# Engine streams written straight into the program, without a block, and the last store waited for last

## The chip, the cores and the metric

The kernel runs on one core of a Trainium2 chip. The metric is the device time of one execution in microseconds. It covers more than the kernel's own instructions: the profiled execution of the kernel before has a span of 169.3 us from its first to its last instruction and a time of 171.16 us.

Three words are used throughout. The *last landing* is the last increment of the semaphore that the last store raises. The *tail* is the time from the last landing to the last record of semaphore 2. No line of the kernel touches semaphore 2; the trace shows its changes before the first and after the last instruction of the program. The *body* is everything up to the last landing.

## The reference

```python
B, H, S, D = 1, 32, 2048, 128            # q, k, v in bfloat16

def reference(q, k, v):
    phi_q = jnp.where(q > 0, q + 1, jnp.exp(q)) + 1e-6
    phi_k = jnp.where(k > 0, k + 1, jnp.exp(k)) + 1e-6
    kv = jnp.einsum("bhsd,bhse->bhde", phi_k, v)
    z = jnp.einsum("bhsd->bhd", phi_k)
    num = jnp.einsum("bhqd,bhde->bhqe", phi_q, kv)
    den = jnp.einsum("bhqd,bhd->bhq", phi_q, z)[..., None] + 1e-6
    return num / den
```

## The kernel before

It works head by head, 32 heads. SyncE issues every load and store. TensorE transposes q, multiplies; ScalarE takes exponentials; VectorE clips, divides and scales; GpSimd does a share of the clipping and copies v. Each operation carries a list of operations that it needs, and a small scheduler turns these into waits on semaphores. For the change only the end matters: how the five lists of instructions get into the program, and what SyncE waits for at last.

```python
NO = 12                                   # output buffers, one semaphore each

def emit(self, eng, engine):
    for fn, waits, name, by in self.plan[eng]:
        for s, v in waits:
            engine.wait_ge(self.get(s), v)
        ins = fn(engine)
        if by:
            ins.then_inc(self.get(name), by)

# ... (head h stores from buffer h % NO and raises semaphore o{h % NO})
        block = es.enter_context(nc.Block())

        @block.gpsimd
        def _(e):
            pr.emit("POOL", e)

        @block.sync
        def _(e):
            pr.emit("SP", e)
            for s in range(NO):
                if f"o{s}" in pr.count:
                    e.wait_ge(pr.get(f"o{s}"), pr.count[f"o{s}"])

        @block.scalar
        # ... and so for TensorE and VectorE
```

## Time and profile before

| | before |
|---|---|
| time, median of the first 3 runs | 171.89 us (171.8 to 172.0) |
| span of the profiled execution | 169.3 us |
| TensorE matmul, VectorE, ScalarE busy | 94%, 91%, 91% of the span |
| DMA: share of the stores' and loads' queue | 98.5% of 16 engines |
| last landing | 168.53 us |
| end of the last instruction | 169.26 us |
| last record of semaphore 2 | 171.17 us |
| tail | 2.64 us |

The first rows say that the body is full and that nothing in it is changed. The last four are read from single records of the trace, since the page rounds to 0.1 us. The lines of the profile are shown with the prediction. In them SP is SyncE, PE TensorE (PEld its weight loads), DVE VectorE, ACT ScalarE and POOL GpSimd; a q behind the name is the engine's sequencer. An EVENT_SEMAPHORE is an instruction that only waits for semaphores or changes them.

### The profile page before, as it was taken

Reading aid. Unit: us, or ns where it says so; the run is one execution under the profiler, and the core shown is the slowest. Engines: PE = TensorE matmul, PEld = TensorE weight load, DVE = VectorE, ACT = ScalarE, POOL = GpSimd, SP = SyncE. Lnnn points to the kernel's source line nnn. Section 1 sums busy time; section 2 is a strip of 40 time slices with the busy share of each in tenths; the row PEclk is TensorE's granted clock in tenths of the full one; section 3 lists DMA queues with packets and bytes.
Section 4 is the critical chain, followed back from the end, with each engine's and each line's share of the span. In section 5 each row is a group of like instructions: output and inputs, shape, how many; then the busy total and the mean of one; then the engine's idle time right before and its main releaser. Section 6 shows DMA issues by size and latency. Waiting matters only on the chain.

```text
span 169.3 us, 6317 instructions
## 1 busy us (share of the span) xinstructions
PE 158.8 (94%) x2775; PEld 153.5 (91%) x2775; DVE 153.5 (91%) x267; ACT 153.7 (91%) x133; POOL 85.8 (51%) x71
## 2 busy tenths in 40 slices
PE   6997999999999999999999999999999999999850
PEld 2576989999999999999999999999999999999740
DVE  0178989999999999999999999999999999999891
ACT  3799989999999999999999999999999999995800
POOL 1446546655665456545566555554565555635000
PEclk9999999999999999999999999999999999999999
DMA  5999999999999999999999999999999999999984
GB/s 204 394 420 415 403 407 410 406 410 410 413 410 410 410 411 407 410 408 419 411 415 417 413 423 411 411 419 408 415 417 414 417 413 419 415 412 420 391 342 175
DMA packets 18748, 67.53 MB, mean 399 GB/s; under 512 B 2080, under 2 KB 2464, under 8 KB 18720
## 3 DMA queue, kind: packets, MB, share of 16 engines
q1 hardware_dynamic: 18720, 67.12, 98.5%
q8 instruction: 22, 0.36, 0.8%
q14 instruction: 6, 0.05, 0.1%
HBM read 50.33 MB, written 16.78 MB: 396 GB/s over the span
## 4 chain that ended last, share of the span: by engine, by line
PE 86%; DVE 6%; ACT 4%; issue 1%; DVEq 0%; POOL 0%; POOLq 0%
PE la L357 33%; PE la L394 19%; PE la L396 17%; PE la L368 15%; DVE la L410 4%; ACT la L336 2%; PE la L315 2%; ACT la L372 1%; PE la L389 1%; DVE la L374 1%; DVE la L403 1%; ACT la L378 1%; DVE la L342 0%; DVEq L253 0%; ACT la L362 0%
## 5 line engine op out<-in xcount | busy, mean ns | idle before, releaser
L410 DVE TENSOR_TENSOR la<-la 128x1536 bf16<-128x1536 f32 (+2 forms) x65 | 77.6, 1195 | 0.3
L396 PE MATMUL la<-la 128*128 128x129 bf16 x512 | 68.1, 220 | 0.0
L394 PE MATMUL la<-la 128*128 128x129 bf16 x512 | 68.1, 219 | 0.0
L372 ACT ACTIVATE la<-la 128x2048 bf16<-128x2048 bf16 (+2 forms) x35 | 60.4, 1731 | 5.0 <-PE la L368 3.3
L357 PE MATMUL la<-la 128*128 128x129 bf16 x1024 | 64.0, 219 | 0.0
L336 ACT ACTIVATE la<-la 128x2048 bf16<-128x2048 bf16 (+1 forms) x33 | 61.3, 1861 | 0.0
L350 POOL COPY la<-la 128x1024 int32<-128x1024 int32 (+1 forms) x33 | 40.3, 1223 | 40.1 <-DVE la L403 30.5
L357 PEld LDWEIGHTS la<-la 128*128 128x128 bf16 x1024 | 60.0, 97 | 0.5 <-POOL la L350 0.5
L346 POOL TENSOR_SCALAR la<-la 128x1024 bf16<-128x1024 bf16 x32 | 44.9, 1403 | 28.2 <-DVE la L410 24.2
L396 PEld LDWEIGHTS la<-la 128*128 128x128 bf16 x512 | 49.5, 97 | 0.0
L394 PEld LDWEIGHTS la<-la 128*128 128x128 bf16 x512 | 47.1, 97 | 0.0
L389 PE MATMUL la<-la 128*128 128x3 bf16 (+1 forms) x192 | 32.3, 168 | 3.4 <-DVE la L410 1.9
L368 PE MATMUL la<-la 128*128 128x128 bf16 x512 | 33.7, 219 | 0.0
L378 ACT ACTIVATE la<-la 128x1024 bf16<-128x1024 bf16 (+1 forms) x32 | 33.5, 1046 | 0.0
L368 PEld LDWEIGHTS la<-la 128*128 128x128 bf16 x512 | 29.2, 97 | 0.9 <-DMA la<-in_q_dram 0.2
L339 DVE TENSOR_SCALAR la<-la 128x2048 bf16<-128x2048 bf16 (+1 forms) x33 | 23.5, 716 | 3.1 <-ACT la L336 3.0
L389 PEld LDWEIGHTS la<-la 128*128 128x128 bf16 x192 | 18.7, 97 | 4.4 <-DVE la L410 2.3
L374 DVE TENSOR_SCALAR la<-la 128x2048 bf16<-128x2048 bf16 (+2 forms) x35 | 21.9, 625 | 0.1
L381 DVE TENSOR_SCALAR la<-la 128x1024 bf16<-128x1024 bf16 x31 | 20.8, 672 | 0.2 <-ACT la L372 0.2
L342 DVE TENSOR_SCALAR la<-la 128x1024 bf16<-128x1024 bf16 x32 | 14.2, 447 | 5.3 <-DMA la<-in_k_dram 5.3
L403 DVE RECIPROCAL la<-la 128x12 f32<-128x12 f32 (+2 forms) x65 | 12.8, 198 | 2.9 <-ACT la L362 1.0
L362 ACT ACTIVATE la<-la 128x129 bf16<-128x129 f32 x32 | 9.0, 282 | 0.8 <-PE la L357 0.8
(14 smaller groups left out, 11.7 us busy)
## 6 DMA issues: line engine op xcount, KB each, us to landing
la<-in_q_dram SPq DMA_DIRECT2D x32, 512.0 KB, 15.4
la<-in_k_dram SPq DMA_DIRECT2D x32, 512.0 KB, 15.3
la<-in_v_dram SPq DMA_DIRECT2D x32, 512.0 KB, 15.4
out_dram<-la SPq DMA_DIRECT2D x31, 512.0 KB, 15.3
out_dram<-la SPq DMA_DIRECT2D x2, 192.0 KB, 2.8
out_dram<-la SPq DMA_DIRECT2D x1, 128.0 KB, 3.0
```

What stands on the lines that cost most here:

```text
L336: add("ACT", f"ek{h}.{i}", lambda e, a=a, b=b: e.activation(em_sb[:, h % NE, a:b], k_sb[:, h % NI, a:b], ACT.Exp), over("ldk", h, ld_parts ...
L346: add("POOL", f"rkp{h}.{i}", lambda e, a=a, b=b: e.tensor_scalar(rk_sb[:, h % NR, a:b], k_sb[:, h % NI, a:b], BIG, 0.0, op0=ALU.min, op1=A ...
L350: add("POOL", f"v1{h}.{i}", lambda e, a=a, b=b: e.tensor_copy(v1_sb[:, h % NV, a:b, 0:D].bitcast(i32), v_sb[:, h % NI, a:b].bitcast(i32)), ...
L357: ins = e.matmul(kv_ps, lhsT=src[:, j], rhs=v1_sb[:, h % NV, j, 0:NC], start=(j + part == 0), stop=(j == NT - 1 and part == 1))
L368: ins = e.transpose(xT[:, j], q_sb[:, h % NI, j], ident[:])
L372: add("ACT", f"eq{h}.{i}", lambda e, a=a, b=b: e.activation(emq_sb[:, h % NQ, a:b], xT[:, a:b], ACT.Exp), over("T", h, t_parts, a, b) + fr ...
L374: add("DVE", f"emq{h}.{i}", lambda e, a=a, b=b: e.tensor_scalar(emq_sb[:, h % NQ, a:b], emq_sb[:, h % NQ, a:b], 1.0, EPS, op0=ALU.min, op1 ...
L378: add("ACT", f"rqa{h}", lambda e: e.activation(rq_sb[:, h % NQ, 0:n], xT[:, 0:n], ACT.Relu), over("T", h, t_parts, 0, n) + freed(NQ, h, (" ...
L389: e.matmul(_ap(o_ps[:, :], o + D, [[NC, m]]), lhsT=ones[:], rhs=epsr[:, 0:m], start=True, stop=False, skip_group_check=True)
L394: e.matmul(to, lhsT=emq_sb[:, h % NQ, t], rhs=kvs_sb[:, h % NK], start=False, stop=False, skip_group_check=True)
L396: ins = e.matmul(to, lhsT=rq_sb[:, h % NQ, t], rhs=kvs_sb[:, h % NK], start=False, stop=True, skip_group_check=True)
L410: return e.tensor_tensor(out=_ap(o_sb[:, :, :, :], first(o_sb[:, h % NO, t0, 0:1]) - first(o_sb[:, :, :, :]), [[m * D, nb], [D, m], [1, D] ...
```

## The change

The intent: a block ends with a drain on each engine, a branch and a barrier of all five engines, and these stand behind the last store. Without a block there is none of it. And since SyncE has to see all twelve output semaphores anyway, the one that comes last is put last.

```diff
-        block = es.enter_context(nc.Block())
-
-        @block.gpsimd
-        def _(e):
-            pr.emit("POOL", e)
-
-        @block.sync
-        def _(e):
-            pr.emit("SP", e)
-            for s in range(NO):
-                if f"o{s}" in pr.count:
-                    e.wait_ge(pr.get(f"o{s}"), pr.count[f"o{s}"])
-        ... (ScalarE, TensorE and VectorE in the same way)
+        for e, engine in (("POOL", nc.gpsimd), ("SP", nc.sync), ("ACT", nc.scalar), ("PE", nc.tensor), ("DVE", nc.vector)):
+            pr.emit(e, engine)
+        last = f"o{(NH - 1) % NO}"
+        for name in [f"o{s}" for s in range(NO) if f"o{s}" in pr.count and f"o{s}" != last] + [last]:
+            nc.sync.wait_ge(pr.get(name), pr.count[name])
```

More of the change, by code (lines that the diff above doesn't have):

```diff
@@ L430, in bass_standalone__linear_attn_elu__prompt_kernel @@
             pr.get(name)
-        block = es.enter_context(nc.Block())
-        @block.gpsimd
-        def _(e):
-            pr.emit("POOL", e)
-        @block.sync
-        def _(e):
-            pr.emit("SP", e)
-            for s in range(NO):
-                if f"o{s}" in pr.count:
-                    e.wait_ge(pr.get(f"o{s}"), pr.count[f"o{s}"])
-        @block.scalar
-        def _(e):
-            pr.emit("ACT", e)
-        @block.tensor
-        def _(e):
-            pr.emit("PE", e)
-        @block.vector
-        def _(e):
-            pr.emit("DVE", e)
+        for e, engine in (("POOL", nc.gpsimd), ("SP", nc.sync), ("ACT", nc.scalar), ("PE", nc.tensor), ("DVE", nc.vector)):
[3 more added lines that the diff above has]
+            nc.sync.wait_ge(pr.get(name), pr.count[name])
 _INS = ['q', 'k', 'v']
```

## The prediction

> **What bounds the kernel now.** I read the page first for the body of the run, then the end of the chain of work, the source views of the two lines that the change deletes, and the run's last microseconds record by record.
>
> ```profile
> span 169.3 us, 6317 instructions
> ...
> PE   6997999999999999999999999999999999999850
> ...
> DVE  0178989999999999999999999999999999999891
> ...
> DMA  5999999999999999999999999999999999999984
> GB/s 204 394 420 415 403 407 410 406 410 410 413 410 410 410 411 407 410 408 419 411 415 417 413 423 411 411 419 408 415 417 414 417 413 419 415 412 420 391 342 175
> ```
>
> The slices of 4.23 us show matmul and the DMA engines at nine tenths from the second slice to about the 37th. Both are full, and the change touches neither. What it touches lies in the last slice, where only stores and waits are left. The chain of waits for the stretch from 162.5 us ends so:
>
> ```profile
> 162.84 0.96 DVE la L410
> 163.80 0.24 DVE la L403 x2
> 164.04 0.86 DVE la L410
> 164.89 0.59 DVEq L253
> ```
>
> The chain stops on VectorE's own drain (L253 is the line of the kernel under which everything at the block's exit is filed) at 165.5 us and does not reach 169.3. So this view does not explain the last 3.8 us: it follows compute, and these 3.8 us are a transfer and semaphore traffic. SyncE's waits and the source views of lines 442 (the wait for the stores) and 253 have them:
>
> ```profile
> SPq L442 <- DMA out_dram<-la: 2.6, 2, 1.3
> ```
> ```profile
> L442 SPq EVENT_SEMAPHORE  x6: 17/28/28, 167.2 to 168.8; - x6
> ```
> ```profile
> L253 POOLq EVENT_SEMAPHORE  x2: 17/17/17, 169.1 to 169.2; - x2
> L253 POOLq DRAIN  x1: 1744/1744/1744, 153.1 to 153.1; - x1
> L253 ACTq DRAIN  x1: 2134/2134/2134, 158.1 to 158.1; - x1
> L253 PEldq DRAIN  x1: 1123/1123/1123, 162.7 to 162.7; - x1
> L253 DVEq DRAIN  x1: 1455/1455/1455, 164.1 to 164.1; - x1
> L253 SPq COMPARE_BRANCH  x1: 38/38/38, 168.9 to 168.9; - x1
> L253 SPq DRAIN  x1: 7/7/7, 169.0 to 169.0; - x1
> L253 SPq EVENT_SEMAPHORE  x1: 17/17/17, 169.2 to 169.2; - x1
> ```
>
> SyncE sits in two waits of 1.3 us, one for head 30's store and one for head 31's. Then come more event semaphores, one branch, a short drain, and the barrier. The four other engines' drains start at 153.1 to 164.1 us and last 1.1 to 2.1 us: all are over by 165.5 us, three microseconds before the last store is in. They look large and cost nothing.
>
> The single records give the tail in ns. The last of the 48 increments of the last store's semaphore comes at 168.532. SyncE's wait that contains it runs 168.549 to 168.577. Four more event semaphores start at 168.622, 168.686, 168.747 and 168.807 (two semaphores each, all long satisfied), the branch, which carries the twelfth wait, at 168.874, the drain at 169.044. GpSimd collects at 169.077 and releases at 169.155; SyncE's last event is 169.197 to 169.214 and TensorE's ends last, at 169.260. The span ends there, but the time doesn't: the profiled run's time is 171.16, and semaphore 2, which no line of the kernel owns, goes on changing: nine records from 169.498 to 170.030 and nine from 170.817 to 171.174, with the clearing of semaphores one after the other between them. So a postamble of 171.174 - 169.260 = 1.91 us follows the kernel and belongs to the time.
>
> **What the Trainium skill says.** "Runtime: NRT & Kernel Launch", section "The ~15µs preamble/postamble breakdown", lists a sync_barrier after the kernel, a clearing of the semaphores and a second sync_barrier, and describes the barrier as a serpentine over five engines at about 44 ns a hop, 355 ns in all. The trace agrees: the nine records before the kernel's first instruction span 0.371 us, those of the second barrier after it 0.357. The first after it takes 0.532, because its second step is 0.212 where the same step elsewhere is 0.038: one engine came late by about 0.17 us. So the program's own barrier is doubled by one that the runtime adds.
> "DMA: Bandwidth & Descriptors", section "Anatomy of one DMA — SWDGE (gpsimd) path", puts most of a transfer's fixed 2 us into the receipt of the last write, and says the engine's semaphore fires after it. Here (another issuing path) the last store is issued at 165.517 and lands 3.0 us later; the last packet ends at 168.189, 0.34 us ahead of the last increment. The change cannot shorten this.
> "ScalarE activation tables: per-element evaluation and per-set limits", section "Table sets in the compiler and the runtime", says the table loads are placed per block. That matters for a rival: without the block, ScalarE's code is no longer a block of its own. The trace has one load, 1.28 us from 0.74 us, right behind the start barrier.
>
> **The change part by part.**
> *The waits behind the last store.* Before, the last store is in slot 31 mod 12 = 7, but its wait isn't the last of SyncE's: from 168.549 to the branch at 168.874 there are five steps, 0.325 us, 65 ns each. With its wait last, the eleven others are spent while the store is in flight. From 165.85 (end of the last issue) to 168.53 there are 2.7 us for them, and eleven at 65 ns are 0.7 us; head 30's store, landing at 167.193, is also among them. All 0.325 us go.
> *The branch.* 168.874 to 169.044, 0.170 us, on the path (38 ns is the branch itself, the rest the gap to the next instruction). It goes. The other engines show no branch at their end.
> *SyncE's drain and the barrier.* From 169.044 to SyncE's release at 169.214: 0.170 us, on the path. It goes. Less the 28 ns of the last wait itself, which stays, SyncE's last instruction ends at 168.577 in place of 169.214: 0.325 + 0.170 + 0.170 - 0.028 = 0.637 us.
> *The other engines' drains.* About 1.1 to 2.1 us each, wholly beside the stores: 0.
> *The runtime's first barrier.* Today all five engines enter it at once, within 50 ns, and it takes 0.532 us with one late engine. I assume the late one is TensorE, which was released last (169.260 against 169.214 to 169.229) and which at the start also had its first instruction at 0.316 where the others had theirs at 0 to 0.138. Without the kernel's barrier, the four engines arrive from 154 to 166 us on and wait there; only SyncE is late. The 0.17 us of the late engine then go: 0.532 - 0.357 = 0.175. I keep SyncE's own 0.284 us from its last instruction to the first hop (169.498 - 169.214), and assume that SyncE starts the serpentine, so that all hops still come after it.
> *Added.* Nothing at run time that I can see. At the start each engine's first instruction already follows the start barrier by 65 ns, so there is no branch into the block to save.
> Sum: 0.637 + 0.175 = 0.81 us, which gives 171.89 - 0.81 = 171.08. In the profile the span should fall by less, 169.260 to 168.577 = 0.68, to 168.6 us.
>
> **The rivals.**
> *The runtime's barrier takes the place of the one removed.* If what counts is only that all engines meet after the last store, then deleting one of two consecutive meetings saves only its own latency. That is what I counted. The stronger form, that the saved time comes back in full as waiting in the runtime's barrier, has against it that SyncE is last in both and simply gets there 0.64 us sooner. It would give 171.8.
> *SyncE isn't first in the serpentine.* Then part of the forward hops are done before SyncE comes, and another 0.04 to 0.2 us go: about 170.9. Nothing in the trace says which engine a record of semaphore 2 belongs to.
> *The waits are not emitted in the written order.* In the trace before they aren't: written as slots 0 to 11, they come as 6, then 7 with 5, 8 with 4, 9 with 3, 10 with 2, 11 with 1, and 0 on the branch. Twelve waits were hung on one instruction and split. The same pattern on the new list would put slot 0 behind the last store, at 65 ns: 171.15. Were the order wholly kept as before, five stay, 0.325 us: 171.4.
> *The table load moves ahead of the start barrier.* If the load is put at the head of the merged code, ScalarE's drain in the start barrier could wait up to 1.28 us for it, and all loads from memory start later. The transfers are full from start to end, so this would be paid at the end: 171.08 + 1.2 = 172.3. For it: loads are placed per block. Against it: the load carries line 372, that of the first activation, so it seems to be placed at that instruction. I give it one chance in fifteen.
> *The trailing waits are lost,* because no instruction follows to carry them. The end would be at SyncE's last issue, 165.85, about 2.7 us earlier still: 168.4, the only way to over 2%. It would be an unsafe kernel, so I hold it at one in a hundred.
>
> **Range and chances.** Of the sum, 0.637 is read from records, 0.175 rests on an assumption, and the likely corrections are 0.1 to 0.2 to either side, with 0.1 for the spread of the runs (171.8 to 172.0). I predict 171.05, a little under 171.08 for the serpentine, and 170.7 to 171.5 eight times in ten. Two per cent is 3.4 us, four times what the change can reach: faster 0.01, within 2% 0.98, slower 0.01.
>
> **What would show it right or wrong.** Right: no record of drain, branch or barrier after 160 us; SyncE's last record is an event semaphore some 20 ns behind the last increment of the last store, which stays near 168.53; the first nine records of semaphore 2 at the end take about 0.36 us from its first to its last, or some lie before 168.5; the second barrier and the clearing unchanged. Wrong: first loads later than 0.74 us or the table load before 0.6 us; event semaphores behind the last increment; the last store landing at a different time by more than 0.2 us, which would mean the body moved, and that I have no reason to expect; a last end of the span near 165.9.

## More of the kernel before

The start matters once, in the spread of the runs: TensorE warms up on matmuls of an identity tile that GpSimd writes first, eight of them (`w2`, `w1`) ahead of the first transposes `T0.0` and `T0.1`.

```python
        def warm(key, n):
            def g(e):
                for w in range(n):
                    ins = e.matmul(o_ps[:, 512:992], lhsT=ident[:], rhs=_ap(ident[:, :], 0, [[0, 4], [1, 120]]), ...)
            add("PE", key, g, ["ident"], inc=False)
```

## The result, and the profile after

The changed kernel took 170.78 us (median of 6 runs, 170.24 to 171.23), the kernel before 171.84 us (6 runs, 171.31 to 172.0). The ratio is 0.9946, with a 95% interval of 0.9921 to 0.9971. Ratios here are the mean time of one kernel's runs over that of the other's runs of the same rounds, so they are not quite the ratio of the medians.

So the kernel became half a per cent faster. The profiled execution looks, at first sight, as if it had not. This is the page after, for the same parts as in the prediction:

```profile
span 169.9 us, 6305 instructions
...
PE   6998699999999999999999999999999999999950
...
DVE  0188989999999999999999999999999999999893
...
DMA  5999999999999999999999999999999999999975
GB/s 200 379 419 413 410 407 407 409 405 407 416 408 409 414 411 408 408 407 417 414 419 412 415 420 411 413 414 410 416 418 421 409 416 421 413 414 417 368 304 203
```

The span is longer, 169.9 for 169.3 us, though it has twelve instructions fewer and its end is cheaper. The chain of waits of the last stretch shows why (columns: start, duration, engine and line):

```profile
164.45 0.96 DVE la L410
165.41 0.24 DVE la L403 x2
165.65 1.45 DVE la L410 x2
```

VectorE's drain, which ended this chain before, is gone. But the same products of the last head, at 162.84 and 164.04 us before, now start 1.61 us later, and the last landing comes at 169.885 for 168.532 us. This one execution has a slower body. The next view says where that began: TensorE's first matmuls (start, duration, count), before and after.

```profile
1.53 3.33 PE L315 MATMUL la<-la 128*128 128x480 bf16 x8 [1.53 <-POOL la L301]
4.70 1.06 PE L368 MATMUL la<-la 128*128 128x128 bf16 x16
```
```profile
1.52 3.38 PE L315 MATMUL la<-la 128*128 128x480 bf16 x8 [1.52 <-POOL la L301]
4.70 1.91 PE L368 MATMUL la<-la 128*128 128x128 bf16 x16
```

Both start the sixteen first transposes at 4.70 us. Before, they take 1.06 us, after 1.91 us: they ran at half the clock. The trace's clock records give full clock from 4.68 us in the one and from 7.43 us in the other. Whether the change did that is a question for the experiments.

The end itself went as the change intends. SyncE's waits for the stores (line 435 after, 442 before):

```profile
SPq L435 <- DMA out_dram<-la: 2.1, 2, 1.6
```
```profile
L435 SPq EVENT_SEMAPHORE  x6: 27/28/28, 168.0 to 169.9; - x6
```

Six event semaphores as before, but the last of them is now the one that waits, and it is the last instruction of all. The view of line 253, where drains, branch and barrier stood, has nothing in it. The single records, both kernels from the last landing on:

| step | before | after |
|---|---|---|
| last landing to the end of SyncE's last instruction | 168.532 to 169.214: 0.682 | 169.885 to 169.929: 0.044 |
| to the last record of semaphore 2's first group | to 170.030: 0.816 | to 170.207: 0.278 |
| clearing of semaphores and semaphore 2's second group | to 171.174: 1.144 | to 171.355: 1.148 |
| tail | 2.642 | 1.470 |

The tail is 1.17 us shorter: 0.64 us inside the program and 0.54 us outside it. The second part is three times what I predicted (0.175). The nine records of the first group say how. Before, they lie together: 169.498, 169.532, 169.744, 169.788, 169.812, 169.909, 169.947, 169.983, 170.030. After, they are torn apart: 165.605, 165.639, 165.677, 167.601, then 170.044, 170.087, 170.125, 170.160, 170.207. Four of the steps were done before the last store had landed.

What the times do not show is the whole 1.17 us: the means of those 6 and 6 runs differ by 0.93 us.

### The profile page after: what moved, and what is told of

Read it like the earlier page. It is cut to its first block, busy times and chain, and to the rows that moved or that the text cites. A ratio compares the mean times of both kernels' runs of the same rounds, so it can differ in the third digit from the quotient of the medians.

```text
span 169.9 us, 6305 instructions
## 1 busy us (share of the span) xinstructions
PE 159.8 (94%) x2775; PEld 154.5 (91%) x2775; DVE 153.8 (91%) x267; ACT 153.8 (90%) x133; POOL 85.4 (50%) x71
## 4 chain that ended last, share of the span: by engine, by line
PE 89%; DVE 6%; ACT 1%; issue 1%; POOL 0%; POOLq 0%
PE la L357 34%; PE la L394 18%; PE la L368 17%; PE la L396 16%; PE la L315 4%; DVE la L410 4%; DVE la L342 1%; ACT la L372 1%; PE la L389 1%; DVE la L403 1%; DVE la L374 0%; POOL la L301 0%; ACT la L362 0%; POOL la L300 0%; POOLq L301 0%
## 5 line engine op out<-in xcount | busy, mean ns | idle before, releaser
L368 PE MATMUL la<-la 128*128 128x128 bf16 x512 | 34.6, 222 | 0.2 <-DVE la L381 0.2
L339 DVE TENSOR_SCALAR la<-la 128x2048 bf16<-128x2048 bf16 (+1 forms) x33 | 22.9, 696 | 3.2 <-ACT la L336 3.1
L381 DVE TENSOR_SCALAR la<-la 128x1024 bf16<-128x1024 bf16 x31 | 21.0, 676 | 0.9 <-ACT la L372 0.5
L342 DVE TENSOR_SCALAR la<-la 128x1024 bf16<-128x1024 bf16 x32 | 15.3, 480 | 5.4 <-DMA la<-in_k_dram 5.4
```

What stands on the lines that cost most here:

```text
L339: add("DVE", f"em{h}.{i}", lambda e, a=a, b=b: e.tensor_scalar(em_sb[:, h % NE, a:b], em_sb[:, h % NE, a:b], 1.0, EPS, op0=ALU.min, op1=AL ...
L368: ins = e.transpose(xT[:, j], q_sb[:, h % NI, j], ident[:])
```

## The experiments

The theory: the tail is a chain of separate terms on SyncE. First the waits behind the last store's own, then branch, drain and barrier, and then the runtime's first barrier, in which the engines take turns in a fixed order and SyncE is fifth. If only SyncE is still missing, just the turn and four return steps follow. Rivals were that the terms are not separate (the order of waits worth nothing by itself, any barrier keeping the runtime's barrier long, the branch rather than the barrier being dear), and that the straight program slows the body. I used the tail as the measure, since it repeats to a few ns while times spread by 0.4 us, and took the times beside it.

### Block kept, last store last: e1_block_last

```diff
             pr.emit("SP", e)
-            for s in range(NO):
-                if f"o{s}" in pr.count:
-                    e.wait_ge(pr.get(f"o{s}"), pr.count[f"o{s}"])
+            last = f"o{(NH - 1) % NO}"
+            for name in [f"o{s}" for s in range(NO) if f"o{s}" != last] + [last]:
+                e.wait_ge(pr.get(name), pr.count[name])
```

> Block and barrier kept, only the order of SyncE's waits changed (last store last). I call tail the time from the last increment of the last store's semaphore to the last record of semaphore 2 (the runtime's): 2.64 us before, 1.47 after the change. Theory (the tail is a chain of separate terms on SyncE): only the four to five steps of 65 ns behind the last store's wait go, tail 2.31 to 2.38, time 0.15 to 0.2% under before. Rival (the order is worth nothing without taking the barrier away, since the compiler regroups the waits anyway): tail 2.64.

Measured: tail 2.383 us, which is 0.26 less. The last store's wait ends at 169.266, and only the branch (169.305), the drain (169.475) and the barrier follow. Time 171.53 against 171.54 us (medians), ratio 0.9996 (0.9971 to 1.0021): a quarter of a us can't be seen in these times. By the trace the order is worth 0.26 us on its own.

### Straight program, slots in the old order: e2_flat_slots

```diff
-        for name in [f"o{s}" for s in range(NO) if f"o{s}" in pr.count and f"o{s}" != last] + [last]:
-            nc.sync.wait_ge(pr.get(name), pr.count[name])
+        for s in range(NO):
+            nc.sync.wait_ge(pr.get(f"o{s}"), pr.count[f"o{s}"])
```

> Straight program, but SyncE waits for the slots in the order 0 to 11 as before, so by the pairing that the trace of the changed kernel shows the last store should stand in the second of six event semaphores. Theory: four steps of 65 ns come back, tail 1.47 + 0.26 = 1.73 us, time 0.15% over the changed kernel. Rival: SyncE's place in the runtime's barrier hides them, tail 1.47.

Measured: tail 1.729 us. SyncE's view limited to the stretch from 169.5 us on:

```profile
L435 SPq EVENT_SEMAPHORE  x5: 28/28/28, 169.9 to 170.1; - x5
```

In the changed kernel the same stretch of the last 0.9 us holds one such instruction:

```profile
L435 SPq EVENT_SEMAPHORE  x1: 28/28/28, 169.9 to 169.9; - x1
```

Four satisfied waits stand behind the one that counted and cost 0.258 us (169.891 to 170.149). They go straight onto the tail; the runtime's barrier does not hide them. Ratio 0.995 (0.9925 to 0.9976). The times do not show the 0.26 us: the mean of these 6 runs, 170.77, is 0.24 us below that of the changed kernel in the same rounds (e4_flat_again below, 171.01), where the tail says 0.26 us above. Spreads of 0.45 and 0.51 us hide it, so this cost rests on the trace alone.

### Barrier put back behind the waits: e3_flat_barrier

```diff
             nc.sync.wait_ge(pr.get(name), pr.count[name])
+        nc.all_engine_barrier()
```

> The changed kernel with an all-engine barrier put back behind the waits, no block and no branch. Theory: the drain and barrier cost 0.17 us on the path plus a gap of 0.04, and the runtime's first barrier goes back from 0.28 to 0.82 us after SyncE's last instruction because all engines enter it together: tail 1.47 + 0.21 + 0.54 = 2.2 us, three quarters of a us lost to the changed kernel. Rival (the branch and the block cost it, or the runtime's barrier became shorter for another reason): tail 1.7 or less.

Measured: tail 2.220 us. Of the 0.75 us that came back, 0.213 are in the program (SyncE's last instruction ends 0.257 us after the landing in place of 0.044) and 0.538 in the runtime's first barrier, which is back at 0.816 to the nanosecond. The view of the barrier's line shows the same pattern as the block's end, less the branch:

```profile
L436 POOLq DRAIN  x1: 2006/2006/2006, 154.3 to 154.3; - x1
L436 ACTq DRAIN  x1: 2134/2134/2134, 159.5 to 159.5; - x1
L436 PEldq DRAIN  x1: 1123/1123/1123, 164.1 to 164.1; - x1
L436 DVEq DRAIN  x1: 1453/1453/1453, 165.4 to 165.4; - x1
L436 SPq DRAIN  x1: 7/7/7, 170.0 to 170.0; - x1
```

The four long drains are over before 167 us; only the 7 ns one lies on the path. Ratio 0.9978 (0.9953 to 1.0003). So the barrier, not the block as such, carries most of the gain. Between this tail and that of e1 lie 0.16 us. They are put down to the branch with the gap behind it, which take 0.170 us in the trace of e1 (169.305 to 169.475); no run adds the branch alone. So the tails form a ladder: 2.64 before, 2.38 with the order changed, 2.22 with the branch gone too, 1.47 without the barrier. In the times the barrier cost 0.36 us against the changed kernel of the same rounds (171.37 for 171.01 in the mean), half of what the tail says, with an error of about 0.28 us.

### The barrier ahead of the waits: e10_barrier_first

```diff
+        nc.all_engine_barrier()
         last = f"o{(NH - 1) % NO}"
```

> The changed kernel with an all-engine barrier, but ahead of SyncE's waits for the stores instead of behind them. Theory (a barrier costs only what of it comes after the last landing, and the runtime's first barrier is short whenever only SyncE is still missing): the engines meet about 0.3 us after the last store is issued, more than 2 us ahead of its landing, and the tail stays at 1.47 us. Rival (any barrier in the program keeps the runtime's barrier long, or resynchronises the engines for it): tail 1.7 to 2.2.

Measured: tail 1.464 us, as without a barrier. SyncE's drain is at 167.5 us and its release at 167.8; the last landing follows at 169.217.

```profile
L433 SPq DRAIN  x1: 122/122/122, 167.5 to 167.5; - x1
L433 SPq EVENT_SEMAPHORE  x1: 17/17/17, 167.8 to 167.8; - x1
```

Four records of semaphore 2 come between 168.095 and 168.385, the other five from 169.373 on. The same barrier that adds 0.75 us to the tail behind the last store adds nothing to it ahead of the landing. Ratio 0.9947 (0.9923 to 0.9972). The rival that any barrier keeps the runtime's barrier long falls.

### Two barriers behind the waits: e11_two_barriers

```diff
             nc.sync.wait_ge(pr.get(name), pr.count[name])
+        nc.all_engine_barrier()
+        nc.all_engine_barrier()
```

> The changed kernel with two all-engine barriers behind the waits. Theory: one barrier behind the waits cost 0.214 us of its own on SyncE (169.938 to 170.152 in the run with one) and 0.54 once, because the engines then enter the runtime's barrier together; the second adds its own 0.21 alone: tail 2.22 + 0.21 = 2.43. Rival (each barrier costs the whole 0.75): 2.97.

Measured: tail 2.541 us, between the two but near the theory. The runtime's barrier is paid once (0.805 us after SyncE's last instruction). The second barrier costs 0.33 us (169.812 to 170.144) where I had 0.21, because TensorE, released last by the first one, has its drain in the second only at 170.0. Ratio 1.0013 (0.9987 to 1.0039): two barriers eat the gain.

### Another engine waits for the last store: e5_wait_pe, e6_wait_pool, e8_wait_dve

The edit is the same three times, with `tensor`, `gpsimd` or `vector`:

```diff
-        for name in [f"o{s}" for s in range(NO) if f"o{s}" in pr.count and f"o{s}" != last] + [last]:
+        for name in [f"o{s}" for s in range(NO) if f"o{s}" in pr.count and f"o{s}" != last]:
             nc.sync.wait_ge(pr.get(name), pr.count[name])
+        nc.tensor.wait_ge(pr.get(last), pr.count[last])
```

> The changed kernel, but TensorE waits for the last store and SyncE for the eleven other slots. Theory (the runtime's first barrier is a serpentine that SyncE enters fifth and TensorE first, so with SyncE last only the turn and four return steps are left to do after the last store): all nine steps come after the landing, tail = 0.07 (wait) + 0.24 (from TensorE's last instruction to the first step, as before) + 0.36 + 1.15 = 1.81 us. Rival (whichever engine is last, the barrier costs the same): tail 1.47 to 1.5.

> The same with GpSimd. If GpSimd is the engine that came 0.17 us late to the third step before (its last instruction at 169.17, the third step at 169.74): tail = 0.04 + 0.57 + 0.29 (third to ninth step) + 1.15 = 2.05 us. If it is second and ScalarE the late third: under 1.95. Rival (the place doesn't matter): 1.5.

> The same with VectorE, which by its 167.60 in the changed kernel's trace (0.50 us after its last product) is the fourth. Tail = 0.03 + 0.2 to 0.5 + 0.24 (fourth to ninth step) + 1.15 = 1.6 to 1.9 us. Rival (the place doesn't matter): 1.5.

| last engine | tail | from its last instruction to its step | records of semaphore 2 ahead of the landing | from its last instruction to the end of the group |
|---|---|---|---|---|
| SyncE (changed kernel) | 1.470 | 0.115 | 4 | 0.278 |
| TensorE | 1.772 | 0.191 | 0 | 0.552 |
| GpSimd | 2.013 | 0.538 | 2 | 0.827 |
| VectorE | 2.063 | 0.629 | 3 | 0.870 |

The number of records ahead of the landing gives the order: TensorE first, GpSimd third, VectorE fourth, SyncE fifth, and so ScalarE second by elimination; no run lets ScalarE wait last. The place matters, and the way from an engine's last instruction to its step matters more: 0.1 us for SyncE, over 0.5 us for GpSimd and VectorE. VectorE's tail was beyond my 1.6 to 1.9, since I had taken at most 0.5 us for that way. That way is no constant of the engine. In the five traces in which VectorE ends with a product and neither a barrier nor an engine ahead of it in the order holds its step (the changed kernel three times, e2, e13), it is 0.50 to 0.53 us, after a wait for the store 0.63. TensorE's is 0.191 us after such a wait and 0.238 after the block's barrier in the trace before. Two of the ratios agree with their tails, 0.9955 (0.9934 to 0.9976) for TensorE and 0.9964 (0.9942 to 0.9987) for GpSimd. VectorE's is 0.994 (0.9917 to 0.9962), lower than its tail explains (0.58 us of 172 would be 0.9966), and its runs happen to have the earliest body of all kernels, 168.8 us in the mean. Of the four engines tried, SyncE is the right one to wait last.

### Both kernels again: e9_before_again, e4_flat_again, e12_flat_third

No edit.

> The kernel before, unedited, against itself: ratio 1 with what the spread allows (0.997 to 1.003). Tail 2.64 +- 0.03. Time less tail (the time of the last landing, called body) is so far 169.04 us in the mean of 23 runs with a block and 169.26 in 24 without. Theory (the body is the same in both, spread by chance): its body is between 168.8 and 169.4, no lower than that of the straight kernels of this call by more than 0.2. Rival (the straight program costs 0.2 us of body): 169.0 here and 169.25 or more in the three others.

> The changed kernel once more, unedited. Its one profile had the last store in at 169.89 us against 168.53 before, with the first transposes taking 1.91 us against 1.06. Theory (a matter of chance in one execution): the last landing falls anywhere between 168.3 and 170 here, tail 1.47 +- 0.05, ratio 0.993 to 0.996. Rival (straight code makes the start slower): first transposes again 1.9 us and last landing again near 169.9 in this run and in the other straight ones.

> The changed kernel a third time, for the size of the gain alone. The tail is 1.17 us shorter in every trace, but the mean time of 12 runs of it is 0.84 us under that of 41 runs of the kernel before (170.89 against 171.73). Theory (what is missing is spread of the body, 0.35 to 0.43 us from run to run): tail 1.47, gain between 0.7 and 1.5 us here, the pooled gain moves toward 1.17. Rival (the straight program costs 0.1 to 0.3 us of body): gain 0.6 to 0.9 again.

| kernel | tail | ratio to before (95%) | full clock from | first transposes | last landing |
|---|---|---|---|---|---|
| before | 2.642 | | 4.68 us | 1.06 us | 168.53 |
| before again | 2.641 | 0.9995 (0.9969 to 1.0021) | 6.52 | 1.91 | 169.63 |
| changed | 1.470 | 0.9946 (0.9921 to 0.9971) | 7.43 | 1.91 | 169.89 |
| changed again | 1.467 | 0.9964 (0.9937 to 0.9991) | 5.16 | 1.28 | 170.04 |
| changed, third | 1.466 | 0.9947 (0.9923 to 0.9971) | 5.66 | 1.52 | 169.62 |

The slow first transposes come with the unedited kernel before too, in this view of its second trace:

```profile
1.53 3.38 PE L315 MATMUL la<-la 128*128 128x480 bf16 x8 [1.53 <-POOL la L301]
4.70 1.91 PE L368 MATMUL la<-la 128*128 128x128 bf16 x16
```

They are therefore not the work of the change. Of what was expected of these three runs, the tails came as said. The changed kernel again had its last landing at 170.04 us, just above my 168.3 to 170, and its ratio of 0.9964 just above 0.993 to 0.996, but its first transposes took 1.28 us and not the 1.9 of the rival. The kernel before again had a body of 169.18 us in the mean, within 168.8 to 169.4; the straight kernels of its call had 169.36, 169.28 and 168.79, the last of which the rival did not allow. The third time the gain was 0.99 us by the means of its rounds, above the rival's 0.6 to 0.9, but the pooled gain moved only from 0.84 to 0.88, as the next figures show. The Trainium skill says on the page "TensorE: Matmul & The Clock Gate", section "What's actually happening", that the clock is raised after a busy window of 3413 ns which runs freely and does not start anew with the kernel. The 14 traces agree that the moment varies: TensorE's work starts at the same 1.5 us in all but one, and full clock comes anywhere from 4.54 to 7.43 us. They do not agree with the size: the same passage puts the variation at 500 ns either way, and here the spread is 2.9 us. Nor does any run show the length of the window; the earliest full clock comes 3.0 us after TensorE's start. In the three traces in which it was there by 4.71 us the last landing was between 168.5 and 169.2 us, in the eleven others between 169.2 and 170.0. That this is the cause of the spread is a correlation, and a weak one: one of the three landed at 169.222 us, later than the 169.217 of e10, whose clock came at 6.75, and the latest landing of all, 170.04, goes with an early clock of 5.16. Among the eleven a later clock does not go with a later landing. No run here sets the moment, and what spreads the body stays open.

How much was gained in time? Over all rounds the kernel before has 52 runs with a mean of 171.76 us (standard deviation 0.37), the changed kernel 18 with 170.88 (0.40). The difference is 0.88 us, and from these spreads its uncertainty is about 0.2 us either way (1.96 times the root of 0.37²/52 + 0.40²/18). The tail says 1.17. So the body of the changed kernel was about 0.3 us later in these runs, which is more than the uncertainty. If I take each run's time less its kernel's tail for all kernels, 56 runs of straight programs (the next experiment left out) have 169.24 us and 58 with a block 169.12: 0.12 us, within 1.96 times the error of 0.075. I could not settle whether the straight program costs a little of the body or whether this is chance. One hint, which was only seen and not tested: the last packet of the stores' queue is followed by the last increment after 0.33 to 0.35 us in all five traces in which the other engines are held until the landing (before, before again, e1, e3, e11), but after 0.94, 0.80 and 0.99 us in the three of the changed kernel. It is no rule: of the kernels whose engines are not held until the landing either, the one with the barrier first, the one in which GpSimd waits and the one of the next experiment have 0.34 to 0.35, and e2, e8 and e5 have 0.43, 0.39 and 0.71.

### Warming on a tile that is ready earlier: e13_warm_on_ones

This is outside the change, an attempt on the start which the traces pointed to.

```diff
-                    ins = e.matmul(o_ps[:, 512:992], lhsT=ident[:], rhs=_ap(ident[:, :], 0, [[0, 4], [1, 120]]),
+                    ins = e.matmul(o_ps[:, 512:992], lhsT=ones[:], rhs=_ap(ones[:, :], 0, [[0, 4], [1, 120]]),
-            add("PE", key, g, ["ident"], inc=False)
+            add("PE", key, g, ["ones"], inc=False)
     "DVE":
-        rkd0.0 v1ones0 em0.0 eps0 em0.1 rkd1.0 rqb0.0 ones emq0.0 ...
+        ones rkd0.0 v1ones0 em0.0 eps0 em0.1 rkd1.0 rqb0.0 emq0.0 ...
```

> An attempt to go below the changed kernel, outside the change: the warming matmuls read the tile of ones, which VectorE writes first, in place of the identity that GpSimd finishes at 1.47 us, so TensorE starts about 0.5 us earlier (1.0 in place of 1.53) and its full clock, seen from 4.5 to 7.4 us in ten traces with earlier landings of the last store where it came by 4.71, should come up to 0.5 us earlier in the mean. Theory: body 0.1 to 0.4 us shorter, time 170.5 to 170.8. Rival (the clock's start doesn't follow TensorE's, or transfers set the body): the same time as the changed kernel of this call within 0.2 us.

```profile
1.05 3.38 PE L315 MATMUL la<-la 128*128 128x480 bf16 x8 [1.05 <-DVE la L308]
4.33 1.31 PE L368 MATMUL la<-la 128*128 128x128 bf16 x16
```

TensorE starts 0.47 us earlier and the first transposes 0.37 us earlier; the tail stays at 1.465. Full clock comes at 4.89 us, within the range of the other traces, so this one trace does not show that the clock came earlier for it. Median 170.54 us (169.82 to 170.97), ratio 0.9925 (0.9896 to 0.9954). Its mean of 170.48 us is 0.37 below the 170.85 of the changed kernel in the same rounds, which with six runs each and deviations of 0.43 and 0.33 is 1.7 times its error of 0.22. This is the fastest kernel and clearly faster than the kernel before; that it beats the changed kernel is likely and not shown.

## Why the prediction was right or wrong

*The waits behind the last store: right.* Predicted 0.325 us. In the trace before, 168.549 to 168.874. Alone, with the block kept, the order is worth 0.26 us, since the block's branch carries one wait and so one step stays; put back into the straight program it costs 0.26.

*Branch and barrier inside the program: right.* Predicted 0.637 us with the waits; measured 0.682 - 0.044 = 0.638.

*The body is full: read a little too simply.* Matmul is not at nine tenths in every slice from the second on: the fourth shows 7. Nothing in the sum rests on it.

*The other engines' drains cost nothing: right.* They stand in e3 and e11 too, beside the stores.

*Nothing is added at the start: right.* The first load is issued at 0.736 us after and 0.738 before, the table load at 0.730 and 0.737. The rival that it moves ahead of the start barrier did not happen.

*No wait was lost, and the pairing:* the rival of reordered waits came half true. The compiler groups the twelve waits in pairs again (slots 6 with 5, 8 with 4, up to the last store's slot 7 with slot 0), but the last store's pair is last, and nothing follows it.

*The runtime's first barrier: the failed step.* I predicted 0.175 us "assume that SyncE starts the serpentine, so that all hops still come after it", and took TensorE for the late engine. Both assumptions are wrong. SyncE is the fifth, and the late one is GpSimd, the third, whose way from its last instruction to its step is 0.54 to 0.57 us when it is last or level with the others. With SyncE alone missing, four of nine steps are done early, and what follows SyncE's last instruction falls from 0.816 to 0.278 us: 0.538 us, three times the term. I had kept SyncE's way to the barrier at 0.284 us; it is 0.115, which is 0.17 us of the difference. The nine records took 0.532 us, and the five that are left take 0.163 (170.044 to 170.207), which is the other 0.37, where I had 0.175. The record would have warned me: I wrote that all five engines enter within 50 ns, but GpSimd's last instruction ends at 169.172, so it is 88 ns, and the engine that I left out is the late one, although its own last instruction ends first. I had this as a rival ("SyncE isn't first in the serpentine") but gave it only 0.04 to 0.2 us beyond the term, because I did not count the engines' own ways to the barrier.

*The sum: too small.* 0.81 us predicted, 1.17 us measured on the tail. By the tail alone the time would have been 171.89 - 1.17 = 170.72 us, at the very edge of the 170.7 to 171.5 that I gave.

*The body: a sign of being wrong that came.* I expected the last landing to stay near 168.53 us and the span to fall to 168.6. It came at 169.89 and the span rose to 169.9. My own list had a landing that moves by more than 0.2 us as a sign of being wrong, since I had no reason to expect it. The first transposes at half clock, which the kernel before shows as well, go with it, but are themselves only 0.85 us longer, for a landing that is 1.35 us later; what moved the body is not shown. Three runs from 171.8 to 172.0 made the body look steadier than it is: its deviation from run to run is about 0.4 us. The time of 170.78 us lay within the range because the tail gained more than I said and the body, in those runs, gave some of it back: that the two errors partly cancel is luck.

## What to carry to other kernels

Account for the end of a program from the last landing on, in single records: every satisfied wait, branch, drain and barrier behind it is paid in full, and a barrier also makes all engines enter the runtime's own barrier together, which here cost more (0.54 us) than the barrier itself (0.21 us). Meetings of the engines belong ahead of the landing of the last store, where they are free; the last wait belongs on SyncE (the best of the four engines tried), as the very last instruction. Judge such a change by the tail in a trace, since a gain of 0.3 us drowns in times that spread by 0.4 us, and don't compare two single spans.

## What the Trainium skill lacked or had wrong

- "Runtime: NRT & Kernel Launch", section "The ~15µs preamble/postamble breakdown", describes the runtime's barrier as a serpentine at about 44 ns a hop, but not the order of the engines. Here TensorE is first, GpSimd third, VectorE fourth and SyncE fifth, and ScalarE second by elimination.
- The same section gives about 1.5 us to the barrier behind the kernel. Here it depends on who comes last: 0.28 us after SyncE's last instruction, 0.55 after TensorE's, 0.83 after GpSimd's, 0.87 after VectorE's, and 0.82 when all come together. Most of the difference is the way from an engine's last instruction to its step (after a wait 0.115 us for SyncE, 0.629 for VectorE), which no page has. Clearing and second barrier took 1.14 to 1.15 us in every trace.
- "DMA: Bandwidth & Descriptors", section "Anatomy of one DMA — SWDGE (gpsimd) path", puts most of a fixed 2 us into the receipt of the last write (it measured another issuing path). Here the whole way from the end of the queue's last packet to the last increment, receipt included, was 0.33 us at the least and 0.99 at the most, and it varied from run to run of one kernel (0.80 to 0.99).
- No page says in what order the compiler puts waits that stand at the end of a stream: here they are grouped two to an event semaphore, by a pattern that isn't the written order, at about 65 ns a step.
